# Two attentions under one gate: exps of the second by a polynomial of degree two, and V products that may begin with 128 columns

## The chip, the core and the metric

The kernel runs on one core of a Trainium2 chip. The metric is the device time of one execution in microseconds (us). A core has TensorE (PE in the profile; PEld is its weight load), VectorE (DVE), ScalarE (ACT), GpSimd (POOL) and SyncE (SP), which run their own instruction streams in order and wait for each other by semaphores. PE writes to PSUM alone, which the kernel divides into four slots of 128 x 1024 float32.

## The reference

```python
def _A_ref(x, wq, wk, wv, wo):            # 32 heads of q, one head of k and v, head size 16
    q = (x @ wq).reshape(B, S, H, Dh).transpose(0, 2, 1, 3)
    k = x @ wk
    v = x @ wv
    p = softmax(einsum("bhqd,bkd->bhqk", q, k) * Dh ** -0.5)
    return einsum("bhqk,bkd->bhqd", p, v).transpose(0, 2, 1, 3).reshape(B, S, H * Dh) @ wo

def _B_ref(x, wqkv, wo):                  # 32 heads of q, k and v
    q, k, v = (x @ wqkv).reshape(B, S, 3, H, Dh).transpose(2, 0, 3, 1, 4)
    p = softmax(einsum("bhqd,bhkd->bhqk", q, k) * Dh ** -0.5)
    return einsum("bhqk,bhkd->bhqd", p, v).transpose(0, 2, 1, 3).reshape(B, S, D) @ wo

g = sigmoid((x * gate_w).sum(-1, keepdims=True))
return g * _A_ref(x, ...) + (1 - g) * _B_ref(x, ...)
```

S = 2048 tokens, D = 512, 32 heads of 16, float32, one batch; both attentions read the same x. The weights are normal with deviation 0.05 (wq and wk of A times 8), so B's scaled scores are small numbers around zero.

## The kernel before

**The work.** Scores are made transposed, keys on partitions, queries on columns, so that exps can go straight into the product with V without a transpose. The work is cut into 8 groups (A and B in turn, eight heads each), and each group into four *phases* (half of the queries, half of the heads): 32 phases. A phase has 32 *quads* (`QUADS`), one for 128 keys and half of the placement in PE's rows; a quad has two *scores*, each 128 x 1024 in one PSUM slot (`products`, eight matmuls of 512 columns that run side by side in PE's sub-arrays). That gives 2048 scores. Each is turned into exps of 128 x 1024 by one instruction, and the quad's two tiles then go through the V product (`values`) into the phase's accumulator, `pair[0]`. The V product of a quad has 512 columns and may be issued in pieces of 128, 256, 384 or 512 (`value_job`). V has a column of ones beside it, so that the row sums of the softmax come out of the same product.

**Who makes exps.** ACT makes most of them (L793). For the others (`vector_job`, `chain`) DVE makes them by arithmetic. For A it goes through the bits of the float and a polynomial (`convert`, `mantissa`, `power`, four times `horner`: five full passes and two at half the time). For B, whose scores are small, it uses a polynomial of degree three in three full passes (`first`, `second`, `third`; L1049, L1052, L1056), with a second tile "w".

**The slots.** One slot is `pair[0]`. Other work that needs PSUM (projections of q, k and v, the output product, turning V, a score for DVE) takes the free slot that `hold()` puts into `pair[1]`; `release()` gives it back. `free["spare"]` is when that slot is free again, and `current` the unit of other work that is under way. Scores for ACT use what is left.

**What sets the order.** Nothing is scheduled at run time. While the program is built, a planner (`_Plan`, `pe_step`) keeps a clock for each engine with rough costs (`EXP`, `PRODUCT`, `SCORES`) and decides what PE issues next: a score, if a slot is free and ACT will want it; or a piece of a V product, or a job of a unit, if it fits in the time until the next score is wanted (`limit`). DVE's work goes into a list (`plan.vec`) with a rank and a due time and comes out by rank. The numbers `CHAIN`, `WORK`, `BEGIN` and the due times only change that order.

**After a phase** (`emptied`, `normalised`): DVE copies the accumulator out (L917), the row sums travel over DRAM into a compact tile (`held`, then `each`, on SP's queue), DVE inverts them and multiplies by the gate (`gated`, L674 and L675), they are spread back by DMA, and DVE multiplies, rounds and splits the result (`times`, `high`, `low`). The output product (`o_unit`) adds two phases of A and two of B; its sums go to DRAM and are added up there.

**The flag.** The fast path is only right for inputs in a range. `stats` gathers maxima; `flag_reduce` and `flag_check` make a flag from them near the end; if it is set, a slow general version runs after.

**The end.** After the last phase the sums are handled by `over`, `times`, `high`, `low` and `products_of` in four pieces of 128 queries, and `give` adds the product to the output row and stores it (L1545). Two of the eight rows go another way: ACT scales them (`added`, L1550) and GpSimd's queue adds them into DRAM.

```python
    def value_job(now, mine, room):
        ...
        m, n = going[mine] if mine in going else (min(can), 0)
        fit = int(min(room, 2 * HALF) // PRODUCT) * P
        wide = min(max(fit, BLK // 2), BLK - n)
```

## Time and profile before

| | |
|---|---|
| median of three runs | 1730.31 us (1729.32 to 1733.89) |
| the profiled execution | 1731.76 us, span 1729.9 us |
| busy | PE 1687.4, PEld 1008.2, DVE 1487.2, ACT 1665.2, POOL 195.5 us |
| first exp starts, last exp starts | 28.2 and 1702.7 us |
| mean granted clock of TensorE | 0.994 |

In rows of groups the figures after `|` are busy us and the mean ns of one instruction, then the engine's idle time before them and what ended it. In rows of the timeline the first number is the start from the span's beginning, the second the length, both us; several instructions that follow each other are one row with their count. A float32 matmul stands in the trace as two, so 16 matmuls of a V product are one piece.

### The profile page before, as it was taken

The numbers are of one execution on the slowest core, as the hardware profiler recorded it, in microseconds if no ns is written. First come the engines' busy times: TensorE is split into PE (matmuls) and PEld (weight loads), VectorE is DVE, ScalarE is ACT, GpSimd is POOL, SyncE is SP. The second block draws the span as 40 slices with busy tenths as digits, with TensorE's granted clock in tenths as the row PEclk, the third lists the DMA queues.
The fourth block names the chain that finished last, engine by engine and source line by source line (L and its number), as shares of the span: only waits on it lengthen the run. The fifth ranks groups of instructions, "written<-read, shape, count | busy, mean of one in ns | idle before, by whom it ended". The sixth has DMA issues, their size and how long they took to land.

```text
span 1729.9 us, 110256 instructions
## 1 busy us (share of the span) xinstructions
PE 1687.4 (98%) x51451; PEld 1008.2 (58%) x51451; DVE 1487.2 (86%) x1658; ACT 1665.2 (96%) x1813; POOL 195.5 (11%) x316
## 2 busy tenths in 40 slices
PE   8999999999999999999999999999999999999996
PEld 5556546456566656666566555665665655655553
DVE  5567699999998899988999888999899898988954
ACT  4999999999999999999999999999999999999994
POOL 1111101000101200011111010111102111111000
PEclk9999999999999999999999999999999999999998
DMA  5212201111212211231222122222213212222312
GB/s 148 74 43 57 56 9 48 41 41 48 54 35 59 68 40 42 53 77 42 41 54 54 48 59 41 47 59 61 60 28 61 59 48 60 36 40 66 121 54 77
DMA packets 71446, 95.72 MB, mean 55 GB/s; under 512 B 27612, under 2 KB 36092, under 8 KB 70980
## 3 DMA queue, kind: packets, MB, share of 16 engines
q1 hardware_dynamic: 53892, 58.61, 12.7%
q0 software_dynamic: 13856, 27.74, 8.0%
q8 instruction: 405, 6.64, 1.6%
q10 hardware_dynamic: 3232, 2.23, 0.4%
q14 instruction: 61, 0.50, 0.1%
HBM read 23.45 MB, written 18.33 MB: 24 GB/s over the span
## 4 chain that ended last, share of the span: by engine, by line
PE 61%; ACT 18%; issue 12%; DVE 7%; DMA 1%; POOL 0%; SPq 0%; ACTq 0%; DVEq 0%; POOLq 0%
PE slot L847 32%; PE slot L762 17%; ACT prob L793 11%; PE slot L215 11%; ACT vec L793 6%; DVE prob L1049 1%; DVE prob L1056 1%; DVE prob L1052 1%; DVE vec L1029 1%; DVE vec L1049 1%; DVE vec L1052 1%; DMA Qa<-hiqa 0%; PE slot L1407 0%; PE slot L309 0%; DVE vec L1016 0%
## 5 line engine op out<-in xcount | busy, mean ns | idle before, releaser
L793 ACT ACTIVATE prob<-slot 128x1024 f32<-128x1024 f32 x1129 | 1121.4, 1101 | 19.3 <-PE slot L762 14.7
L793 ACT ACTIVATE vec<-slot 128x1024 f32<-128x1024 f32 x657 | 685.6, 1099 | 7.6 <-PE slot L762 3.6
L847 PE MATMUL slot<-prob,vB 64*32 64x256 f32 (+3 forms) x8096 | 529.6, 439 | 0.1
L847 PE MATMUL slot<-prob,vA 64*32 64x512 f32 (+3 forms) x7536 | 499.1, 447 | 0.0
L762 PE MATMUL slot<-Qa,kA 64*32 64x512 f16 x8192 | 441.6, 378 | 8.4 <-DMA Qa<-hiqa 2.0
L762 PE MATMUL slot<-Qb,K 64*32 64x512 f16 x8192 | 421.2, 378 | 12.7 <-ACT prob L793 4.6
L847 PE MATMUL slot<-vec,vB 64*32 64x512 f32 (+3 forms) x4640 | 367.8, 434 | 0.8 <-issue 0.7
L847 PE MATMUL slot<-vec,vA 64*32 64x512 f32 (+3 forms) x4656 | 365.7, 446 | 0.0
L762 PEld LDWEIGHTS <-K 64*32 64x32 f16 x8192 | 192.4, 90 | 239.9 <-issue 191.3
L762 PEld LDWEIGHTS <-kA 64*32 64x32 f16 x8192 | 191.8, 90 | 235.4 <-issue 180.8
L847 PEld LDWEIGHTS slot<-prob,vB 64*32 64x32 f32 x8096 | 214.9, 106 | 38.8 <-issue 8.5
L847 PEld LDWEIGHTS slot<-prob,vA 64*32 64x32 f32 x7536 | 199.8, 106 | 43.4 <-issue 14.0
L847 PEld LDWEIGHTS slot<-vec,vB 64*32 64x32 f32 x4640 | 144.7, 106 | 26.6 <-issue 8.3
L847 PEld LDWEIGHTS slot<-vec,vA 64*32 64x32 f32 x4656 | 140.2, 106 | 26.4 <-issue 8.3
L1049 DVE TENSOR_SCALAR prob<-slot 128x1024 f32<-128x1024 f32 x109 | 133.0, 1220 | 17.9 <-PE slot L762 15.1
L1029 DVE SCALAR_TENSOR_TENSOR prob<-prob,prob 128x1024 f32<-128x1024 f32 x83 | 101.1, 1220 | 1.0
L1049 DVE TENSOR_SCALAR vec<-slot 128x1024 f32<-128x1024 f32 x71 | 86.6, 1220 | 12.4 <-PE slot L762 8.2
L215 PEld LDWEIGHTS <-o 64*32 64x32 f16 x3072 | 56.5, 93 | 32.8 <-ACT o L694 6.8
L1016 DVE TENSOR_SCALAR prob<-slot 128x1024 int32<-128x1024 f32 x46 | 56.2, 1221 | 19.4 <-PE slot L762 17.0
L1052 DVE SCALAR_TENSOR_TENSOR prob<-prob 128x1024 f32<-128x1024 f32 x59 | 71.5, 1219 | 0.5
L1056 DVE SCALAR_TENSOR_TENSOR prob<-prob,prob 128x1024 f32<-128x1024 f32 x59 | 71.5, 1218 | 0.2
L1029 DVE SCALAR_TENSOR_TENSOR prob<-prob,vec 128x1024 f32<-128x1024 f32 x55 | 67.0, 1220 | 0.7
(190 smaller groups left out, 1748.5 us busy)
## 6 DMA issues: line engine op xcount, KB each, us to landing
vB<-vB SPq DMA_DIRECT2D x32, 192.0 KB
prob<-back SPq DMA_DIRECT2D x184, 32.0 KB
out_dram<-vec POOLq DMA_DIRECT2D x36, 128.0 KB, 4.7
xT<-out_dram SPq DMA_DIRECT2D x16, 256.0 KB
out_dram<-prob POOLq DMA_DIRECT2D x28, 128.0 KB, 4.3
out_dram<-prob SPq DMA_DIRECT2D x24, 128.0 KB
out_dram<-xT SPq DMA_DIRECT2D x12, 256.0 KB
vec<-in_A_x_dram SPq DMA_DIRECT2D x10, 256.0 KB
```

The costliest lines, as they stand in the source:

```text
L215: nc.tensor.matmul(outs[n : n + COLS, i], lhs[i][rows(i), n : n + COLS], rhs[i][rows(i)], start=start, stop=stop)
L762: nc.tensor.matmul(bank[a : a + COLS, hh], k[rows(hh), key : key + COLS], Q[src, gi, half, p][rows(hh), j * BLK : (j + 1) * BLK], start=Tr ...
L793: nc.scalar.activation(probs[u], sc, AF.Exp, scale=SCALE / (UP * UP))
L847: nc.tensor.matmul(pair[0][32 * k : 32 * k + 32, i, cols], v[rows(i)], probs[2 * m + k // 2][rows(i), hh, cols], start=first, stop=last)
L1016: nc.vector.tensor_scalar(tile("p").bitcast(I32), pair[1], SCALE / (UP * UP) / math.log(2) * 2.0 ** 23, None, op0=ALU.mult)
L1029: nc.vector.scalar_tensor_tensor(p, m if i == 3 else p, VEC[i], m if i else w, op0=ALU.add, op1=ALU.mult)
L1049: nc.vector.tensor_scalar(tile("p"), pair[1], CUBE[0] * SCALE / (UP * UP), CUBE[1], op0=ALU.mult, op1=ALU.add)
L1052: nc.vector.scalar_tensor_tensor(tile("w"), tiles["p"], CUBE[2], tiles["p"], op0=ALU.add, op1=ALU.mult)
L1056: nc.vector.scalar_tensor_tensor(p, w, CUBE[3], p, op0=ALU.add, op1=ALU.mult)
```

## The change

Six things change.

1. **B's exps on DVE** become a polynomial of degree two in two passes: the score is scaled to p, and then (p + constant) x p is made. The polynomial's constant, about 1, is left out of the tile. The tile "w" is no longer needed. Only in the last phase is the constant added by a pass of its own (`third`).
2. **The constant comes back later.** For each half of a V projection, `sums_of` sums v over each 64 keys (a reduction from PSUM, a small multiplication, two transfers). When a B phase is normalised, `missing` adds up the sums of those quads that DVE made; `gated` adds the count to the row sums and `times` adds the sum to the result.
3. **The limit.** B's scores must stay under 0.044 instead of 0.16, so the bound is now by norms: `norms` squares q and k of B (before, `magnitudes` took magnitudes of q alone) and a small matmul adds them by head; `flag_pairs` multiplies the largest norms of q and k by head. This makes 16 such jobs instead of 8; B's k loses its plain maximum.
4. **V products** may begin with 128 columns, where before a first piece had at least 256, if the slot of other work is taken and no unit is under way (`least`).
5. **Numbers of the planner** change: `CHAIN` 28000 for A, `WORK` 500, `BEGIN` 4, tiles kept free, due times and earliest starts.
6. **The end**: all eight rows of the last part go through `give`; `added` is gone.

In the built order the counts are:

| | before | after |
|---|---|---|
| exps on ACT | 1796 | 1766 |
| exps on DVE: B, A | 180, 72 | 228, 54 |
| V products: pieces of 128, 256, 384, 512 columns | 330, 420, 330, 484 | 525, 475, 479, 296 |
| norm jobs on PE (L522, now L564) | 8 | 16 |

PE, in a phase of A near the beginning. `Qa00` are queries, `kA` keys, `slot` the PSUM slots, `vA` V, `prob` and `vec` the exps; one V piece is two rows. Before, a piece of 256 columns that begins a quad:

```order
L215 LDWEIGHTS w16vb01_780
L215 MATMUL slot3_82<-xT_83,w16vb01_780 32x512
L847 MATMUL slot2_81<-prob6_102,vA0_88 32x256 x4
L847 MATMUL slot2_81<-vec0_106,vA0_88 32x256 x4
L762 LDWEIGHTS kA_87
L762 MATMUL slot0_79<-Qa002_363,kA_87 32x512
```

and after, a place where a quad's last 256 columns are followed by the first 128 of the next, and then by a score:

```order
L816 LDWEIGHTS kA_87
L816 MATMUL slot1_80<-Qa002_366,kA_87 32x512
L901 MATMUL slot3_82<-vec4_110,vA1_89 32x256 x4
L901 MATMUL slot3_82<-vec3_109,vA1_89 32x256 x4
L901 MATMUL slot3_82<-vec2_108,vA0_88 32x128 x4
L901 MATMUL slot3_82<-prob0_96,vA0_88 32x128 x4
L816 LDWEIGHTS kA_87
L816 MATMUL slot2_81<-Qa003_367,kA_87 32x512
```

The interval between two scores there holds three units of 128 columns; before, a remainder of one unit could not be filled by a new quad.

DVE, from the copy that empties the accumulator of the 13th phase, the first of the second group of B. `slot` to `prob` or `vec` begins a chain. Before, the next 24 rows up to `gated` (L674) begin

```order
L917 COPY prob2_98<-slot1_80 128x1024
L1049 TENSOR_SCALAR vec2_108<-slot2_81 128x1024
L1052 SCALAR_TENSOR_TENSOR prob5_101<-vec2_108 128x1024
L1056 SCALAR_TENSOR_TENSOR vec2_108<-prob5_101,vec2_108 128x1024
L1049 TENSOR_SCALAR prob3_99<-slot3_82 128x1024
L247 TENSOR_SCALAR w16oa10_18034<-woa1_18032 128x512
L1052 SCALAR_TENSOR_TENSOR vec3_109<-prob3_99 128x1024
L250 SCALAR_TENSOR_TENSOR w16oa10_18034<-woa1_18032,w16oa10_18034 128x512
```

and after, all rows up to `gated` (L724 adds the count to `each`, L725 inverts it) are

```order
L972 COPY prob9_105<-slot1_80 128x1024
L1104 TENSOR_SCALAR prob7_103<-slot2_81 128x1024
L1107 SCALAR_TENSOR_TENSOR prob7_103<-prob7_103 128x1024
L1104 TENSOR_SCALAR prob2_98<-slot2_81 128x1024
L225 TENSOR_REDUCE stats_86<-w16kb20_18695 128x1
L1107 SCALAR_TENSOR_TENSOR prob2_98<-prob2_98 128x1024
L569 TENSOR_REDUCE stats_86<-slot2_81 64x1
L248 TENSOR_SCALAR w16ob10_18920<-wob1_18918 128x512
L545 TENSOR_REDUCE lost300_18975<-sums1_15233 64x1 x2
L724 TENSOR_SCALAR each300_18962<-each300_18962 128x32
L725 RECIPROCAL each300_18962<-each300_18962 128x32
```

Chains are two rows long instead of three, and `gated` has moved from the 24th row behind the copy to the ninth.

DVE at the very end, `give` in before (L1545) and after (L1620):

```order
L689 SCALAR_TENSOR_TENSOR vec1_107<-vec1_107 128x128
L1545 SCALAR_TENSOR_TENSOR xT_83<-slot1_80,gate_up_95,xT_83 128x512
L697 TENSOR_TENSOR o16712_43733<-vec1_107,o16712_43733 128x128
L689 SCALAR_TENSOR_TENSOR vec1_107<-vec1_107 128x128
L1545 SCALAR_TENSOR_TENSOR xT_83<-slot1_80,gate_up_95,xT_83 128x512
L697 TENSOR_TENSOR o16712_43733<-vec1_107,o16712_43733 128x128
L1545 SCALAR_TENSOR_TENSOR xT_83<-slot3_82,gate_up_95,xT_83 128x512 x2
L1545 SCALAR_TENSOR_TENSOR xT_83<-slot2_81,gate_up_95,xT_83 128x512 x2
```

```order
L1620 SCALAR_TENSOR_TENSOR xT_83<-slot3_82,gate_up_95,xT_83 128x512
L751 TENSOR_TENSOR o16712_45360<-vec2_108,o16712_45360 128x128
L740 SCALAR_TENSOR_TENSOR vec2_108<-vec2_108 128x128
L1620 SCALAR_TENSOR_TENSOR xT_83<-slot3_82,gate_up_95,xT_83 128x512
L751 TENSOR_TENSOR o16712_45360<-vec2_108,o16712_45360 128x128
L1620 SCALAR_TENSOR_TENSOR xT_83<-slot0_79,gate_up_95,xT_83 128x512 x2
L1620 SCALAR_TENSOR_TENSOR xT_83<-slot2_81,gate_up_95,xT_83 128x512 x2
L1620 SCALAR_TENSOR_TENSOR xT_83<-slot1_80,gate_up_95,xT_83 128x512 x2
```

The first two `give` now read the tile of the first 128 queries, which was ACT's; two more stand at the end.

The diff, cut to its core (line numbers of before are in the kernel above):

```diff
-B_MAX = 0.16
+B_MAX = 0.044
-CUBE = (0.5500864384102879, 0.8808852829622843, -0.986763876, 1.22848465)
+SQUARE = (1.0000001191795511, 1.0002430729569356, 0.4999387172344313)
...
             one = plan.vec(hi, 1130, 1, t + TO_VEC)
+            if part == "v":
+                one = plan.vec(blocks, 1250, 0, 0.0, (one,))
             plan.vec(lo, 1130, 0, 0.0, (one,), then)
...
+    def sums_of(gi, half):
+        if half == 0:
+            v_sums[gi] = ops.tile([P, 2, 2 * NT], F32, tag="sums", name=f"sums{gi}", bufs=2)
+        at = slice(NT * half, NT * (half + 1))
+        own, other = v_sums[gi][:, 0, at], v_sums[gi][:, 1, at]
+        nc.vector.tensor_reduce(own, pair[1].rearrange("p e (n k) -> p (e n) k", k=ROWS), axis=AX.X, op=ALU.add)
+        nc.vector.tensor_scalar(own, own, SQUARE[0] * UP ** -2, None, op0=ALU.mult)
+        swapped(other, own, nc.sync)
+        plan.sp += 2 * ISSUE_SP
...
+    def missing(ph, to):
+        n, half, q = phases[ph]
+        sums = v_sums[n // 2]
+        taken = [divmod(m - 32 * ph, 2) for m in range(32 * ph, 32 * ph + 32) if m in vector]
...
+                nc.vector.tensor_reduce(to[rows(i), r : r + 1], sums[rows(i), i ^ (q // 2), a:b], axis=AX.X, op=ALU.add)
...
-        nc.vector.tensor_scalar(mag.bitcast(I32), hi.rearrange("p e t -> p (e t)").bitcast(I32), 0x7FFF7FFF, None, op0=ALU.bitwise_and)
+        nc.vector.tensor_scalar(mag, hi, -HI_MAX, HI_MAX, op0=ALU.max, op1=ALU.min)
+        nc.vector.scalar_tensor_tensor(mag, mag, SQUARED / (UP * UP), mag, op0=ALU.mult, op1=ALU.mult)
...
         def gated():
+            if short:
+                count = missing(ph, lost)
+                nc.vector.tensor_scalar(each, each, SQUARE[0] * ROWS * count, None, op0=ALU.add)
             nc.vector.reciprocal(each, each)
...
-        plan.vec(gated, 430, 3.5, now + 7500, (), spreads, min(due, now + 25000),
+        plan.vec(gated, 900 if short else 430, 3.5, now + 7500, (), spreads, min(due, now + 35000),
...
-        wide = min(max(fit, BLK // 2), BLK - n)
+        least = P if n == 0 and free["spare"] > now and not current else BLK // 2
+        wide = min(max(fit, least), BLK - n)
...
             def first():
-                nc.vector.tensor_scalar(tile("p"), pair[1], CUBE[0] * SCALE / (UP * UP), CUBE[1], op0=ALU.mult, op1=ALU.add)
+                nc.vector.tensor_scalar(tile("p"), pair[1], math.sqrt(SQUARE[2]) * SCALE / (UP * UP), None, op0=ALU.mult)
             def second():
-                nc.vector.scalar_tensor_tensor(tile("w"), tiles["p"], CUBE[2], tiles["p"], op0=ALU.add, op1=ALU.mult)
+                nc.vector.scalar_tensor_tensor(tiles["p"], tiles["p"], SQUARE[1] / math.sqrt(SQUARE[2]), tiles["p"], op0=ALU.add, op1=ALU.mult)
             def third():
-                p, w = tiles["p"], tiles["w"]
-                nc.vector.scalar_tensor_tensor(p, w, CUBE[3], p, op0=ALU.add, op1=ALU.mult)
-                give("w")
+                nc.vector.tensor_scalar(tiles["p"], tiles["p"], SQUARE[0], None, op0=ALU.add)
...
-    CHAIN = 14000, 7000
-    JOB, AFTER, TURN, WORK = 500, 3000, 3000, 2500
+    CHAIN = 28000, 7000
+    JOB, AFTER, TURN, WORK = 500, 3000, 3000, 500
...
+    def flag_pairs():
...
-        elif t == 2:
-            give(1, 0)
         else:
-            give(1, 1)
+            give(0, t - 2)
         low[t]()
         products_of(t)
-        if t in (1, 2):
-            added(0, t - 1)
-    for t in (2, 3):
+    for t in range(1, 4):
         for e in range(2):
             give(t, e)
```

## The prediction

> **What bounds the kernel now.** I read the page first, then the busy times of the stretch in which exps run, then the timeline of single stretches, and last the groups by form. The page:

> ```profile
> span 1729.9 us, 110256 instructions
> ...
> PE 1687.4 (98%) x51451; PEld 1008.2 (58%) x51451; DVE 1487.2 (86%) x1658; ACT 1665.2 (96%) x1813; POOL 195.5 (11%) x316
> ...
> PEclk9999999999999999999999999999999999999998
> ```

> TensorE (PE) and ScalarE (ACT) both look full, VectorE (DVE) nearly so; a busy PE is not a PE at its peak, so the 98% decides nothing. The view of stretches and the source view of the exp line give the stage that matters, from the first exp to the end of the last; the columns of the stretch are span, then busy us and count of PE, PEld, DVE, ACT and POOL.

> ```profile
> 28.20:1703.80 1675.60, 1654.51 (x50809) 989.20 (x50817) 1462.39 (x1602) 1655.08 (x1797) 189.04 (x302) 1.00 0.22 52
> ```

> ```profile
> L793 ACT ACTIVATE prob<-slot x1129: 1016/1103/1257, 28.2 to 1702.7; 128x1024 f32<-128x1024 f32 x189
> L793 ACT ACTIVATE vec<-slot x657: 1014/1103/1223, 37.9 to 1700.8; 128x1024 f32<-128x1024 f32 x165
> ```

> ACT is busy for 1655.1 of 1675.6 us. With ten more into borrowed tiles (`early`, `vB`) its exps are 1796. What one costs, and what PE's work costs, is read from a piece of timeline near the end where both run without a gap:

> ```profile
> 1698.14 1.97 ACT L793 ACTIVATE prob<-slot 128x1024 f32<-128x1024 f32 x2
> 1699.94 2.00 ACT L793 ACTIVATE vec<-slot 128x1024 f32<-128x1024 f32 x2
> 1701.75 2.02 ACT L793 ACTIVATE prob<-slot 128x1024 f32<-128x1024 f32 x2
> ```

> ```profile
> 1700.31 0.41 PE L762 MATMUL slot<-Qb,K 64*32 64x512 f16 x8
> 1700.53 0.85 PE L847 MATMUL slot<-prob,vB 64*32 64x384 f32 x16
> 1701.17 0.42 PE L762 MATMUL slot<-Qb,K 64*32 64x512 f16 x8
> 1701.39 0.85 PE L215 MATMUL slot<-w16oa,o 64*32 64x512 f16 x24
> 1702.04 0.42 PE L762 MATMUL slot<-Qb,K 64*32 64x512 f16 x8
> 1702.25 0.42 PE L847 MATMUL slot<-prob,vB 64*32 64x128 f32 x16
> 1702.47 1.07 PE L847 MATMUL slot<-vec,vB 64*32 64x512 f32 x16
> 1703.33 1.07 PE L847 MATMUL slot<-prob,vB 64*32 64x512 f32 x16
> ```

> Two exps take 1.805 us from start to start (1698.14 to 1699.94 to 1701.75), so one costs 0.903; I use 0.905. PE works in units: a score is one (1700.31 to 1700.53, 0.22), a projection or output step one (24 matmuls in 0.65 are three), 128 columns of a V product one (1702.25 to 1702.47, 0.22; 384 columns 0.64; 512 columns 0.86). I use 0.2155 a unit. Counted in the built order, before has 2048 scores, 4096 units of V and 1158 jobs of other work (some 30 of them counted as two or three units by their matmuls): 7349 units, 1583 us. ACT's 1796 exps are 1625 us. In 1675.6 us ACT thus loses 50 us and PE 92. ACT is the bound; PE is 4.09 units an exp, 0.882 us against 0.905, close behind. Where ACT loses its 50 us the table of waits names PE:

> ```profile
> ACT prob L793 <- PE slot L762: 14.7, 19, 6.4
> ...
> ACT vec L793 <- PE slot L762: 3.6, 10, 0.8
> ```

> That is ACT waiting for a score that PE gave late; the rest are smaller delays.

> **The exps.** Of 2048 exps, DVE makes 252 before (180 of source B, 72 of A). In the built order after, it makes 228 of B and 54 of A, 282, and ACT 1766. ACT loses 30 exps: 30 x 0.905 = 27.2 us less. This lies on the path.

> **DVE.** What it pays, by the groups:

> ```profile
> L1049 DVE TENSOR_SCALAR prob<-slot 128x1024 f32<-128x1024 f32 x109 | 133.0, 1220 | 17.9 <-PE slot L762 15.1 <-ACT prob L793 1.8 <-ACT vec L793 0.7
> ...
> L1052 DVE SCALAR_TENSOR_TENSOR prob<-prob 128x1024 f32<-128x1024 f32 x59 | 71.5, 1219 | 0.5
> ...
> L1020 DVE TENSOR_SCALAR prob<-prob 128x1024 int32<-128x1024 int32 x29 | 20.1, 691 | 0.6
> ...
> L224 DVE TENSOR_REDUCE stats<-hikb 128x1 f32<-128x1024 f16 x8 | 9.7, 1208 | 0.0
> ```

> ```profile
> L516 DVE TENSOR_SCALAR vec<-hiqb x5: 417/418/421, 178.4 to 1576.2; 128x512 int32<-128x512 int32 x5
> ```

> A B chain falls from three passes of 1.22 to two; an A chain stays at five of 1.22 and two of 0.69. Full passes: 180 x 3 + 72 x 5 = 900 before, 228 x 2 + 54 x 5 = 726 after, -174 x 1.22 = -212 us; 36 fewer of 0.69, -25. Added: the constant's own pass for six exps of the last phase (L1110), 4 us at 0.69; eight reductions for the V sums, 10 us at 1.21; eight more norm reductions against eight fewer maxima of k, nothing. The two new passes over 16 norms against eight of 0.42 are not in the trace: between 0.42 + 1.22 (nearest row: the same bytes) and 2 x 1.22 each, 23 to 36 us; I take 23. The small sums of the missing constant: 15 times some four operations, each at most the 0.35 of L674's row below, so 0 to 21 us; I take 10. Together some -190, so DVE goes to about 1300 of 1487 us. None of that is a gain by itself: the cover is that a score whose exp DVE makes is asked for ahead of need. The eight more norm jobs each hold a PSUM bank for a unit and a reduction; the scores keep the two that they have in such a hold anyway, so I cost that at nothing beyond the units. If the cover goes, ACT waits (third rival).

> **PE gives some back.** Work stays (7357 units, with eight more norm jobs), so it is now 4.17 units an exp, 0.898 us against 0.905. To price it I split the built order at every eighth score that goes to ACT and took for each stretch the larger of 8 x 0.905 and its units x 0.2155. The sum is 1642.2 before and 1622.6 after, -19.6. Split at every third score, which leaves nearly no buffer, it is 1666.3 and 1654.1, -12.3; at every 64th, -23.5; ACT alone, -27.2. The measured 1675.6 lies above all of these, so what is between is lost in either kernel to waits that the count doesn't know. I take -19.6, since stretches of 8, 5 and 16 agree within 2 (-20.2 at 5, -21.2 at 16), and keep -12 and -27 as ends. The shorter first piece of V is in these counts: 525 pieces of 128 columns instead of 330, 1775 pieces instead of 1564. Intervals between two scores with exactly four units grow from 870 to 1083, those with five or more fall from 567 to 483.

> Does a piece cost more than its columns? The row at 1702.25 says not: 0.22 us for 128 columns, a quarter of 0.86. [...]

> **The late `gated`.** After each phase DVE copies the accumulator out, the row sums travel by DMA (`held`, then `each`), and DVE inverts them (L674). Before, in a B phase:

> ```profile
> 719.08 1.23 DVE L917 COPY prob<-slot 128x1024 f32<-128x1024 f32 x1 [0.38 <-PE slot L847]
> ...
> 745.37 0.35 DVE L674 RECIPROCAL each<-each 128x32 f32<-128x32 f32 x1
> ```

> Here 25 us of chain work stand between. In the order after, at the same phase, nine operations stand there, four full passes of 1.22, a reduction of 1.21 and small ones, some 7 us. The transfer has no other cover, and DVE runs in order, so it may stand idle. One event of before shows the price:

> ```profile
> 1558.92 0.35 DVE L674 RECIPROCAL each<-each 128x32 f32<-128x32 f32 x1 [2.86 <-DMA each<-held]
> ```

> ```profile
> 1557.74 1.03 ACT L793 ACTIVATE prob<-slot 128x1024 f32<-128x1024 f32 x1
> 1560.73 1.02 ACT L793 ACTIVATE vec<-slot 128x1024 f32<-128x1024 f32 x1 [1.96 <-DVE prob L1056]
> 1562.45 1.03 ACT L793 ACTIVATE prob<-slot 128x1024 f32<-128x1024 f32 x1 [0.69 <-PE slot L762]
> 1564.15 1.02 ACT L793 ACTIVATE prob<-slot 128x1024 f32<-128x1024 f32 x1 [0.68 <-PE slot L762]
> 1565.71 1.02 ACT L793 ACTIVATE prob<-slot 128x1024 f32<-128x1024 f32 x1 [0.53 <-PE slot L762]
> ```

> Four exps took 7.97 us (1557.74 to 1565.71) instead of 3.62, 4.35 lost. In all of before DVE waited for this transfer twice among 31 inversions, 3.2 us together (a row of the view of tile `each`):

> ```profile
>   DMA each<-held: 3.2, 2
> ```

> So most waits should be short and hidden by the score that lies ready; I take +1 in all, between 0 and 4.35 for each of 15 phases. The 16 new transfers of V sums on SP, 0.58 of issue each by the row of that queue below, are used a phase or more later: nothing, unless they push `each` back, which is the same rival. The two transfers for the flag (about 10 of its small operations on DVE) have 40 us of distance planned: nothing.

> **The tail.** Two output rows that ACT and GpSimd made are made by DVE now.

> ```profile
> 1715.67 0.69 ACT L1550 ACTIVATE prob<-slot,gate_up 128x512 f32<-128x512 f32 x1 [0.40 <-PE slot L215]
> ...
> 1716.95 0.75 DVE L1545 SCALAR_TENSOR_TENSOR xT<-slot,gate_up,xT 128x512 f32<-128x512 f32 x1 [0.81 <-PE slot L215]
> ...
> 1718.88 2.72 DVE L1545 SCALAR_TENSOR_TENSOR xT<-slot,gate_up,xT 128x512 f32<-128x512 f32 x4
> ```

> ```profile
> 1710.50 0.58 SPq L659 DMA_DIRECT2D vec<-prob  x1
> ```

> Two more of 2.72 / 4 = 0.68 are +1.36; the wait of 0.81 goes, since the tile that DVE now takes first was ready for ACT at 1715.67. Net +0.5. Two more issues on SP (0.58) run beside them. The wider bound is -0.8 to +1.4.

> **The sum.** -19.6 + 1.0 + 0.5 = -18.1. The profiled execution took 1731.8 us, 1.9 of them around its span; less 18.1 it is 1713.7. It lies 1.5 above the median of the three runs (1730.3), so a median near 1712. A change under 0.3% (5.2 us) can't be told from none.

> **Rivals.**
> First, PE becomes the bound outright: it keeps the 92 us that it loses now and gets 8 more units (+1.7), with the tail +0.5: 1730.3 + 2.2 = 1732.5, the same. For it speaks that 0.898 is within 1% of 0.905; against it that much of those 92 us is the remainder of 0.905 after four units (0.043 each), and that fewer intervals are now uneven.
> Second, weight loads no longer hide behind short pieces. The weight load's mean is 106 ns in

> ```profile
> L847 PEld LDWEIGHTS slot<-prob,vB 64*32 64x32 f32 x8096 | 214.9, 106 | 38.8 <-issue 8.5 <-ACT prob L793 0.4 <-DVE prob L917 0.4
> ```

> and one bare load for each of 211 more pieces is 22 us: 1712 + 22 = 1734, the same. The row at 1702.25 speaks against it.
> Third, slower: DVE waits for `each` in the B phases. Its place is the new `gated` ahead of which 7 us of work stand, its price 4.35 an event; from 1712 it needs six events of the 15 to pass 1735.5, and seven give 1742. For it speaks the lost 25 us of cover; against it that two waits in 31 inversions is all that before shows, and that DVE has spare time to catch up.
> Fourth, better: the event at 1558 does not come back (-4.35) and the 128 columns fill what PE lost, so the full -27.2 stands: 1699.
> That the fast path is left for the general one can be excluded: with these inputs the largest scaled product of a head's norms is 0.039, under the new limit of 0.044.

> **Chances.** Forecast (1703 to 1722) 0.70, PE bound 0.08, weight loads 0.04, DVE waits 0.08, better 0.10. Faster 0.80, same 0.12, slower 0.08. The range leaves out the slower rival and the two at 1732 to 1734: 1699 to 1723.

> **What the profile after would show.** ACT with 1766 exps at 0.905 and a stretch from first to last exp near 1657 us; DVE near 1300 us busy; V pieces of 128 columns still at 0.22 from start to start; DVE's waits for `each` under 1 us apiece; last exp to end 26.5 us instead of 26.1. I am wrong if ACT's waits for PE's scores grow by more than 10 us, if pieces of 128 columns are spaced wider, or if the waits for `each` reach ACT.

## The result and the profile after

The changed kernel is slower: 1742.93 us (median of 8 runs, 1738.28 to 1749.26) against 1730.64 (8 runs on the same chip), a ratio of 1.0065 with a 95% interval of 1.004 to 1.0089. Forecast were 1712 us and a range of 1699 to 1723. The profiled execution took 1745.55 us. Runs in which TensorE was granted a lower mean clock than the usual 0.992 to 0.997 took longer (of e10 below, one at 0.986 took 1710 us and the others 1692 to 1697), and e11 can't be understood without that.

The page of the changed kernel, the parts on busy time, on DMA queues and on the chain that ended last:

```profile
span 1743.7 us, 116765 instructions
...
PE 1694.9 (97%) x54859; PEld 1109.9 (64%) x54859; DVE 1336.7 (77%) x1568; ACT 1654.0 (95%) x1781; POOL 194.1 (11%) x314
...
PEclk9999999999999999999999999999999999999998
...
q8 instruction: 431, 7.06, 1.7%
...
PE 83%; ACT 7%; DVE 5%; issue 2%; DMA 1%; SPq 0%; ACTq 0%; DVEq 0%
```

The same two parts of the page of before, which the prediction did not look at:

```profile
q8 instruction: 405, 6.64, 1.6%
...
PE 61%; ACT 18%; issue 12%; DVE 7%; DMA 1%; POOL 0%; SPq 0%; ACTq 0%; DVEq 0%; POOLq 0%
```

ACT and DVE did what was forecast: 1766 exps on ACT instead of 1796, and the durations of all DVE instructions add up to 1402 us instead of 1584 (busy time counts overlapping ones once, so it fell by 150 only). But TensorE has 3408 matmuls and as many weight loads more, and the chain that ended last now runs over PE for 83% of the span instead of 61%. ACT's waits, of the table of waits (total, times, longest):

```profile
ACT prob L847 <- PE slot L816: 24.5, 46, 5.2
ACT vec L847 <- PE slot L816: 13.5, 28, 1.5
```

These are 38.0 us in 74 waits for scores, where before had 18.3 in 29. From the starts of the exps: beyond 0.904 an exp ACT lost 51.7 us between its first and last exp before, and 94.2 after. That is 42.5 more: it eats up the 27.2 us of the 30 exps and 15 us besides. No single event stands out. By size, the delays of 0.1 to 0.3 us add 18 us (156 instead of 44), those of 0.3 to 1 us 21 (75 instead of 35) and longer ones 5.

How PE came to be late stands in a piece of the timeline, in source A:

```profile
1307.23 1.23 PE L901 MATMUL slot<-prob,vA 64*32 64x512 f32 x16
...
1308.09 0.59 PE L816 MATMUL slot<-Qa,kA 64*32 64x512 f16 x8
1308.30 0.83 PE L901 MATMUL slot<-prob,vA 64*32 64x384 f32 x11
1308.84 1.03 ACT L847 ACTIVATE prob<-slot 128x1024 f32<-128x1024 f32 x1
1310.20 0.52 PE L901 MATMUL slot<-prob,vA 64*32 64x384 f32 x3 [1.06 <-issue]
...
1311.32 1.02 ACT L847 ACTIVATE vec<-slot 128x1024 f32<-128x1024 f32 x1 [1.45 <-PE slot L816]
```

A V product of 384 columns stops in its middle, after 11 of its 16 matmuls, and goes on at 1310.20 with no releaser named but "issue". One such place proves little, since the program has a few waits inside pieces too. The records of queue q8 show what else happens there: a packet of 16 KB starts at 1306.94 and lands at 1308.90, 1.30 us before PE goes on. All packets of q8 are 16384 bytes: 7.06 MB in 431. For 2 x 54859 weight loads and matmuls that is 64.4 bytes each, and before it was 64.5 (405 packets for 2 x 51451). So a packet would hold some 254 instructions of TensorE; I take blocks of 256, which e4 below shows by its stops. That makes 26 blocks more after. Between 100 and 1700 us there are 72 places where over 0.5 us lie from one matmul's start to the next; 42 of them end 1.25 to 1.75 us after such a block landed; before it was 12 of 52. By chance it would be about one in eight, for blocks come 4.0 us apart on average after and 4.25 before.

That gives the theory: **TensorE can be short of instructions.** Blocks seldom come closer than some 3.4 us (1% of the distances are under 3.33 us and 5% under 3.44 after, 3.38 and 3.50 before), so there are seldom more than about 75 instructions a us. A score or a step of other work has 16 instructions in 0.2155 us, 74 a us; a V piece has 32 whatever its width, so 512 columns are 37 a us, 256 are 74, and 128 are 149. A score and 384 columns fill 0.862 us with 48 instructions; a score, 128 and 256 columns fill the same time with 80, which is 93 a us. The rivals: the new order is worse for another reason (norm jobs, limits of the planner, bank holds), and the blocks only stand by; a piece has a fixed price, such as a weight load that is not hidden; DVE's waits for the row sums.

### The profile page after: what moved, and what is told of

Read it like the earlier page. It is cut to its first block, busy times and chain, and to the rows that moved or that the text cites. A ratio compares the mean times of both kernels' runs of the same rounds, so it can differ in the third digit from the quotient of the medians.

```text
span 1743.7 us, 116765 instructions
## 1 busy us (share of the span) xinstructions
PE 1694.9 (97%) x54859; PEld 1109.9 (64%) x54859; DVE 1336.7 (77%) x1568; ACT 1654.0 (95%) x1781; POOL 194.1 (11%) x314
## 3 DMA queue, kind: packets, MB, share of 16 engines
q8 instruction: 431, 7.06, 1.7%
## 4 chain that ended last, share of the span: by engine, by line
PE 83%; ACT 7%; DVE 5%; issue 2%; DMA 1%; SPq 0%; ACTq 0%; DVEq 0%
PE slot L901 45%; PE slot L816 23%; PE slot L216 14%; ACT prob L847 4%; ACT vec L847 3%; DVE prob L1104 1%; DVE vec L1104 1%; DVE prob L1107 1%; SPq L702 0%; DVE vec L1107 0%; PE slot L1482 0%; DMA each<-held 0%; PE slot L587 0%; DVE xT L1620 0%; DMA vec<-in_A_x_dram 0%
## 5 line engine op out<-in xcount | busy, mean ns | idle before, releaser
L847 ACT ACTIVATE prob<-slot 128x1024 f32<-128x1024 f32 x1091 | 1072.6, 1064 | 30.7 <-PE slot L816 24.5
L847 ACT ACTIVATE vec<-slot 128x1024 f32<-128x1024 f32 x665 | 676.7, 1061 | 20.3 <-PE slot L816 13.5
L901 PE MATMUL slot<-prob,vB 64*32 64x128 f32 (+3 forms) x8960 | 540.7, 402 | 4.2 <-issue 3.6
L901 PE MATMUL slot<-prob,vA 64*32 64x128 f32 (+3 forms) x8544 | 518.9, 419 | 1.8 <-issue 1.8
L816 PE MATMUL slot<-Qa,kA 64*32 64x512 f16 x8192 | 494.8, 378 | 6.4 <-issue 1.9
L901 PE MATMUL slot<-vec,vB 64*32 64x384 f32 (+3 forms) x5696 | 400.2, 401 | 1.3 <-issue 1.0
L901 PE MATMUL slot<-vec,vA 64*32 64x128 f32 (+3 forms) x5080 | 360.6, 414 | 1.6 <-issue 1.1
L901 PEld LDWEIGHTS slot<-prob,vB 64*32 64x32 f32 x8960 | 255.1, 106 | 53.2 <-issue 15.3
L901 PEld LDWEIGHTS slot<-prob,vA 64*32 64x32 f32 x8544 | 235.8, 106 | 45.9 <-issue 17.3
L901 PEld LDWEIGHTS slot<-vec,vB 64*32 64x32 f32 x5696 | 179.0, 106 | 30.5 <-issue 10.0
L1107 DVE SCALAR_TENSOR_TENSOR prob<-prob 128x1024 f32<-128x1024 f32 x146 | 178.5, 1223 | 3.2
L901 PEld LDWEIGHTS slot<-vec,vA 64*32 64x32 f32 x5080 | 160.7, 106 | 27.3 <-issue 8.7
L1104 DVE TENSOR_SCALAR vec<-slot 128x1024 f32<-128x1024 f32 x82 | 100.0, 1220 | 13.6 <-PE slot L816 10.8
L1107 DVE SCALAR_TENSOR_TENSOR vec<-vec 128x1024 f32<-128x1024 f32 x82 | 100.3, 1223 | 1.7
L1084 DVE SCALAR_TENSOR_TENSOR prob<-prob,prob 128x1024 f32<-128x1024 f32 x71 | 86.8, 1222 | 1.6
L216 PE MATMUL slot<-w16ob,o 64*32 64x512 f16 x1536 | 65.3, 391 | 5.6 <-ACT o L748 5.1
```

The source lines that it names most:

```text
L216: nc.tensor.matmul(outs[n : n + COLS, i], lhs[i][rows(i), n : n + COLS], rhs[i][rows(i)], start=start, stop=stop)
L816: nc.tensor.matmul(bank[a : a + COLS, hh], k[rows(hh), key : key + COLS], Q[src, gi, half, p][rows(hh), j * BLK : (j + 1) * BLK], start=Tr ...
L847: nc.scalar.activation(probs[u], sc, AF.Exp, scale=SCALE / (UP * UP))
L901: nc.tensor.matmul(pair[0][32 * k : 32 * k + 32, i, cols], v[rows(i)], probs[2 * m + k // 2][rows(i), hh, cols], start=first, stop=last)
L1084: nc.vector.scalar_tensor_tensor(p, m if i == 3 else p, VEC[i], m if i else w, op0=ALU.add, op1=ALU.mult)
L1104: nc.vector.tensor_scalar(tile("p"), pair[1], math.sqrt(SQUARE[2]) * SCALE / (UP * UP), None, op0=ALU.mult)
```

## Experiments

### The rule alone, undone and done

e1 is the changed kernel without the short beginning; e2 is the kernel before with it and nothing else.

```diff
 e1 (from the changed kernel)
-        least = P if n == 0 and free["spare"] > now and not current else BLK // 2
+        least = BLK // 2
 e2 (from the kernel before)
+        least = P if n == 0 and free["spare"] > now and not current else BLK // 2
-        wide = min(max(fit, BLK // 2), BLK - n)
+        wide = min(max(fit, least), BLK - n)
```

> The changed kernel with the one rule undone that lets a V product begin with 128 columns: it begins with 256 again. In the built order 1620 pieces of V instead of 1775 (1564 before), ACT with 1772 exps instead of 1766. Instruction theory: the extra pieces cost TensorE instructions, not columns; with them gone some 412 instruction blocks of 16 KB instead of 431, ACT's waits for PE's scores back near 20 us, and the sum of the prediction holds: 1710 to 1722 us. Rival, the new order as a whole (norm jobs, shorter chains, limits of the planner) is worse and the blocks only stand by: 1738 to 1748, as with the rule. Rival, waits of DVE for the row sums: also 1738 to 1748.

> The kernel before with that one rule added and nothing else: 1735 pieces of V instead of 1564, ACT's 1796 exps as before. Instruction theory: slower than before by 5 to 25 us, some 426 blocks instead of 405, and ACT's waits for PE's scores at 30 us or more instead of 18. Rival, the new order as a whole: 1726 to 1734, no change. By columns alone (the prediction's step): no change or a little faster, since TensorE fills time that it lost.

Measured: e1 1733.26 us, ratio to before 1.0002 (0.9988 to 1.0016); e2 1784.75 us, 1.0295 (1.0264 to 1.0325). The short beginning by itself costs 50 us in the old order and some 10 in the new one. The direction is the instruction theory's: e2 fetched 426 blocks, and ACT's waits for scores went from 18.3 to 44.5 us. The 50 us are twice the most that was expected, so a count of blocks alone doesn't give the price. e1 does not fit: it should have gained 10 to 20 us, and gained nothing. ACT has 24 exps fewer there and loses 73.5 us beyond 0.904 an exp instead of 51.7. The page and the waits of e1:

```profile
PE 1690.3 (98%) x52379; PEld 1019.9 (59%) x52379; DVE 1332.8 (77%) x1574; ACT 1646.5 (95%) x1787; POOL 190.9 (11%) x314
...
q8 instruction: 412, 6.75, 1.7%
```

```profile
ACT prob L847 <- PE slot L816: 22.1, 30, 5.3
...
ACT vec L847 <- PE slot L816: 6.1, 15, 0.9
ACT prob L847 <- PE slot L901: 5.0, 4, 1.7
...
ACT vec L847 <- PE slot L901: 3.0, 2, 1.5
```

The waits for scores are 28.2 us, ten more than before, with 7 blocks more. The last two rows have grown: ACT waits for V products (L901) to empty its tiles, 8.0 us in 6 waits against 2.5 in 2 before and 3.7 in 6 after. Three of them, of 1.5 us, come in source-A phases some 417 us apart (at 617, 1034 and 1451 us), where a phase ends just as a q projection has filled the other bank: V stands until DVE has copied the accumulator. A second loss follows each some 10 us later, and the six together cost ACT 11 us. That comes of the order, and it takes a part of the gain that e1 should have had. The third rival of the prediction shows up here once as well: before the last inversion, at 1662.6 us, DVE waits 7.5 us for `each`, and 5 us later ACT waits 3.0 us for `back`, the transfer that follows.

### More instructions, nothing else

e3 and e4 keep the order of before and every column where it was; V pieces are only issued in shorter calls.

```diff
-            values(m, slice(n, n + wide))
 e3: 384 columns as 128 and 256
+            cuts = [n, n + P, n + wide] if wide == 3 * P else [n, n + wide]
+            for x, y in zip(cuts, cuts[1:]):
+                values(m, slice(x, y))
 e4: all pieces as 128
+            for x in range(n, n + wide, P):
+                values(m, slice(x, x + P))
```

> The kernel before in its own order, each V piece of 384 columns issued as 128 and 256 back to back: same columns, same places, 330 more pieces, some 10600 more TensorE instructions, some 41 more blocks. Instruction theory: at least 12 us slower, ACT's waits for PE's scores doubled. Columns alone: 1728 to 1733, no change. A bare weight load a piece: 330 x 0.106, 35 us slower.

> The kernel before in its own order, every V piece issued as pieces of 128 columns: 4096 pieces instead of 1564, some 184000 TensorE instructions instead of 103000, about 719 blocks. Instruction theory: blocks come no faster than one in about 3.4 us (the shortest distances in the traces of before and after), so 719 x 3.4 = 2440 us. Columns alone: 1731 us. A bare weight load a piece: 2532 x 0.106 = 268, about 2000 us.

Measured: e3 1802.42 us (1.0412, 1.0384 to 1.0441), e4 2778.53. "Columns alone" is dead: the same columns in the same places cost 1044 us more in e4 (one run, at a clock of 0.986, against 1734.08 of before on the same chip). In e3 ACT's waits for scores went from 18.3 us in 29 to 61.1 in 106. The instruction theory had the direction; for e4 it said 2440 us, for it reckoned 3.4 us a block, and the 721 blocks came 3.84 us apart on average. The timeline of PE in e4 shows the mechanism by itself:

```profile
1504.89 0.27 PE L847 MATMUL slot<-vec,vA 64*32 64x128 f32 x1 [1.58 <-issue]
1504.90 0.31 PE L847 MATMUL slot<-prob,vA 64*32 64x128 f32 x4
1504.93 0.45 PE L762 MATMUL slot<-Qa,kA 64*32 64x512 f16 x4
1505.03 0.29 PE L847 MATMUL slot<-prob,vA 64*32 64x128 f32 x4
1505.14 0.60 PE L762 MATMUL slot<-Qa,kA 64*32 64x512 f16 x11
1505.37 0.27 PE L847 MATMUL slot<-prob,vA 64*32 64x128 f32 x2
1505.38 0.38 PE L762 MATMUL slot<-Qa,kA 64*32 64x512 f16 x1
1505.38 0.70 PE L847 MATMUL slot<-prob,vA 64*32 64x128 f32 x26
1505.84 0.42 PE L762 MATMUL slot<-Qa,kA 64*32 64x512 f16 x4
1505.90 0.30 PE L847 MATMUL slot<-prob,vA 64*32 64x128 f32 x4
1506.01 0.40 PE L762 MATMUL slot<-Qa,kA 64*32 64x512 f16 x4
1506.06 0.79 PE L847 MATMUL slot<-prob,vA 64*32 64x128 f32 x32
1506.73 0.41 PE L762 MATMUL slot<-Qa,kA 64*32 64x512 f16 x8
1506.95 0.62 PE L847 MATMUL slot<-vec,vA 64*32 64x128 f32 x23
1508.64 0.62 PE L847 MATMUL slot<-vec,vA 64*32 64x128 f32 x26 [1.07 <-issue]
```

Add the counts from one "issue" row to the row ahead of the next: 128 matmuls, so with their weight loads 256 instructions, one block. PE runs them in 2.7 us and stands until the next is there, 3.75 us after the last; both stops cut a piece in two. Of the 682 gaps over 0.5 us in e4, 509 end 1.25 to 1.5 us after a block landed, and 542 of the 681 stretches between them have exactly 128 matmuls. The gaps add up to 1064 us, about what e4 lost. Of the two queues of kind "instruction" only q8 grew in e4, from 405 to 721 packets (q14 has 61 in both); for the 2532 x 32 instructions that the edit gave TensorE that is 63.9 bytes each.

**A sum with instructions.** The prediction's count can now be mended. Over stretches of four ACT scores take the largest of 4 x 0.905, units x 0.2155 and instructions x 3.8 / 256 us, and add up. The 3.8 is e4's; the four was chosen because it fits the six stretches of exps known by then (unlike the prediction's count it leaves out the work behind the last full stretch, so its level is some 7 to 10 us lower):

| | before | after | e1 | e2 | e3 | e4 |
|---|---|---|---|---|---|---|
| blocks counted | 398 | 425 | 406 | 420 | 440 | 715 |
| without instructions, us | 1644 | 1625 | 1633 | 1647 | 1644 | 1644 |
| with them, us | 1668 | 1695 | 1667 | 1717 | 1746 | 2708 |
| measured, first to last exp's start, us | 1674 | 1690 | 1675 | 1727 | 1742 | 2715 |

Without the third term it gives the prediction's gain, 19 us; with it, a loss of 27, where 15 were measured. The sign does not hang on the four: counted again in the built order at stretches of 3, 5, 8 and 16, the loss is 27, 29, 22 and 25. It has e1 level with before, as was measured. The next runs tested it on kernels that it had not seen.

### Where instructions are added

All three keep the order of before.

```diff
 e5: scores of source A in two halves of 256 columns, 16 matmuls instead of 8
+                step = BLK // 2 if src == "a" else BLK
+                for x in range(0, BLK, step):
+                    nc.tensor.matmul(bank[a : a + COLS, hh, x : x + step], ...
 e6 (w = 4) and e7 (w = 2): pieces of 512 or of 256 columns in two halves
+            step = wide // 2 if wide == w * P else wide
+            for x in range(n, n + wide, step):
+                values(m, slice(x, x + step))
```

> The kernel before in its own order; each score of source A is issued as 8 matmuls of 256 columns and 8 more of the other 256, so 16 weight loads and 16 matmuls instead of 8 and 8. V pieces are untouched; 16400 more TensorE instructions, 64 more blocks. Instruction theory, by a sum over stretches of four ACT scores, each the largest of 4 x 0.905, units x 0.2155 and instructions x 3.8 / 256 us (it gives 1668, 1695, 1667, 1717, 1746, 2708 for the stretch of exps of before, after, e1, e2, e3 and e4, where 1674, 1690, 1675, 1727, 1742, 2715 were measured): +160, about 1890 us. Theory that a V piece has a fixed price of about 0.2 us, whatever its neighbours: no change, 1731. Columns alone: 1731.

> The kernel before in its own order; each V piece of 512 columns is issued as 256 and 256: 484 more pieces, 61 more blocks, and in the place where they lie TensorE has at most 74 instructions a us. Instruction theory by the sum: +91, about 1822 us. Fixed price of a piece (70 us for 330 pieces in e3, 0.21 each): +103, 1833; this run alone tells little between the two, the pair with the next one does. Columns alone: 1731.

> The kernel before in its own order; each V piece of 256 columns is issued as 128 and 128: 420 more pieces, 53 more blocks, fewer than in the run before. Instruction theory by the sum: +146, about 1877 us, dearer than the run before though fewer pieces are added, because these double the instructions where TensorE has 149 a us. Fixed price of a piece: 420 x 0.21 = +88, 1819, cheaper than the run before. Columns alone: 1731.

Measured: e5 1901.24 us, e6 1825.20, e7 1848.01, against 1731.96 before: +169, +93 and +116 where the sum said +160, +91 and +146. e5 touches no V piece and costs the most, so it is no price of V pieces. e7 adds fewer pieces than e6 and costs more, so a piece had no fixed price: it cost 0.19 us in e6, whose halves have 74 instructions a us by the count above, and 0.28 in e7, whose halves have 149. The waits of e7:

```profile
ACT prob L793 <- PE slot L762: 69.1, 102, 6.2
...
ACT vec L793 <- PE slot L762: 29.7, 53, 1.3
```

### A cheaper order that was not

```diff
 e8 (from the changed kernel)
-LEFT, LEFT_END, BEGIN = 1, 1, 4
+LEFT, LEFT_END, BEGIN = 2, 1, 4
...
-        least = P if n == 0 and free["spare"] > now and not current else BLK // 2
+        least = BLK // 2
```

> The changed kernel with V beginning with 256 columns, and two spare tiles instead of one kept back before a burst of other work: 1577 pieces, 401 blocks, ACT with 1786 exps. Instruction theory by the sum: 1664 for the stretch of exps against 1668 of before, so 1724 to 1731 us. By the prediction's count without instructions: 1637 against 1644, about the same gain, so this run only asks whether a cheaper order beats both kernels.

Measured: 1739.80 us, ratio 1.0045 (1.0029 to 1.006): a miss by 9 to 16 us. The sum knows no banks and no full tiles; in e8 ACT waits for V products again, 5.3 us in 6 waits, and for scores 28.2. Differences under some 12 us are beyond it. Of the runs with all products, none beats the kernel before.

### Fewer instructions

If instructions are the limit, the change should pay once they are not. In these kernels the V products of the second 64 rows are left out, except in the first and last quad of a phase. The two row halves run side by side: in before, the 512 columns at 1702.47 are eight matmuls and, 0.43 us later, eight more; in e9 the 512 columns at 1670.88 are four and, also 0.43 us later, four more. So the columns of the first 64 rows and their places stay, and a V piece has 16 instructions instead of 32. e9 is before, e10 after, e11 is e1 and e12 is e2, all with this edit.

```diff
-            for i in range(2):
+            for i in range(2 if put_in[0] in (0, QUADS - 1) else 1):
```

> The kernel before in its own order, but in all V quads of a phase except the first and the last, the products of the second 64 rows are left out. The two row halves run beside each other on TensorE, so a piece should still take 0.2155 us per 128 columns with half the instructions: some 307 blocks instead of 398. Instruction theory by the sum: 1655 instead of 1668 for the stretch of exps, about 1718 us. Columns alone: 1731. It is the base for the next two.

> The changed kernel with the same products left out: some 321 blocks instead of 425. Instruction theory by the sum: 1634 for the stretch, 21 below the run before, so about 1697 us: the gain that was predicted comes out once instructions don't limit. Rival, the new order itself is worse: 10 to 15 us above the run before, as it is with all products.

> The changed kernel with V beginning with 256 columns and the same products left out: 311 blocks. Instruction theory by the sum: 1643, 12 below e9 and 9 above e10, so about 1706 us: the short beginning, which costs 10 with all products, gains here. Rival, the order: level with e9, as it is with all products.

> The kernel before with the short beginning alone (as in e2) and with the V products of the second 64 rows left out as in e9. With all products the short beginning cost 2.95%. Instruction theory by the sum: 1659 for the stretch of exps against 1655 in e9, so about 1722 us, a ratio of 0.993 to the kernel before where e9 had 0.9905. Rival, the order that the short beginning makes is bad in itself: some 50 us above e9, a ratio near 1.02.

| | median us | ratio to before | interval | with all products |
|---|---|---|---|---|
| e9 (before) | 1718.83 | 0.9905 | 0.9890 to 0.9921 | 1 |
| e10 (after) | 1694.61 | 0.9781 | 0.9751 to 0.9810 | 1.0065 |
| e11 (e1) | 1724.48 | 0.9905 | 0.9872 to 0.9938 | 1.0002 |
| e12 (e2) | 1726.57 | 0.9955 | 0.9939 to 0.9972 | 1.0295 |

e9 and e10 came within 3 us of what was expected, and e10 is 24.2 us faster than e9; expected were 21. The same change in the same order costs 12 us with 425 blocks and gains 24 with 321. So the order is not bad in itself, and the price of the short beginning in the old order falls from 50 us to 8 (e12 over e9, where the sum said 4 and the rival some 50). A rival would be that these kernels also relieve PE of columns, since the other 64 rows stand free. A score's matmuls do start earlier beside a V piece (after a piece of 512 columns the next operation starts at 0.72 us in e9 instead of 0.86), but PE goes through the columns of the first 64 rows no faster: over stretches of 100 units the quickest 1% take 0.215 us a unit in e9 and 0.214 in e10, against 0.217 before and 0.216 after. The page and the waits of e10:

```profile
PE 1655.3 (98%) x41539; PEld 991.6 (59%) x41539; DVE 1332.7 (79%) x1568; ACT 1634.7 (97%) x1781; POOL 194.0 (11%) x314
...
q8 instruction: 327, 5.36, 1.4%
```

```profile
ACT prob L847 <- PE slot L816: 8.3, 5, 6.0
ACT vec L847 <- PE slot L816: 2.5, 4, 1.0
```

74 waits for scores have become 9. e11 missed its 1706 us. By its median it is level with e9, as the rival had it. Four of its six runs had a granted clock of 0.986 or 0.987 and took 1724 to 1726 us; the two at 0.994 and 0.995, the clock of e9's runs, took 1712 and 1710, 7 to 9 below e9 and 15 to 17 above e10. The profiled one is of the four: its clock was down near the end (0.58 on average from 1645 to 1676 us). By the two runs alone the short beginning gains in the new order once instructions don't limit, but 11 of the 15 to 17 us are the losses around ends of phases that e1 has: they are still there in e11 (three of 1.74 us and three of 1.96), so they come of the order and not of instructions. In the old order the short beginning still costs 8 us. What it is worth by itself is thus not settled.

## Why the prediction was wrong

- **The exps and DVE: right.** 1766 ACT exps, 927 of them still 0.90 to 0.91 us behind the one ahead; DVE's durations fell by 182 us (forecast 190; its busy time is 1336.7 us, forecast near 1300), and none of it was a gain by itself.
- **"Does a piece cost more than its columns?": this step failed.** The prediction answered from the row at 1702.25, 0.22 us for 128 columns, that the 211 extra pieces were free. The row is right, and half of the 128-column pieces that run whole in the changed kernel still take 0.218 us or less, but it stands beside 512-column pieces, which need 37 instructions a us. What the pieces brought was 211 x 32 = 6752 instructions, 26 blocks of q8. The page of before had q8 with 405 packets, and the planner's `takes` counts 32 a piece and 16 a step against `BLOCK` and `READ` (256 and 3400 ns); either was a reason to count instructions as well as columns. (The planner's 3.4 us a block is itself too short: in e4 it was 3.84.)
- **"PE gives some back", -19.6: mis-sized for the same cause.** It took the larger of two terms where there are three. With the third it is +27 by the sum, +15 measured in the stretch, and +12.3 in the medians where the whole sum said -18.1. The gain that it named exists: 24 us between e9 and e10.
- **First rival, PE bound at 1732.5:** the engine was right (83% of the chain), the size not. It kept PE's loss of 92 us; PE's loss grew to 105 (1690.8 less 7357 units of 0.2155).
- **Second rival, weight loads no longer hidden, 1734:** its total was nearer than the forecast, its mechanism not. A bare load for each piece gives about 2000 us in e4 (2778 measured) and a price by the piece, which e6 against e7 excludes. Nor would e4's PE, at a price by the piece, run 128 matmuls in 2.7 us and then stand.
- **Third rival, waits for `each`:** they grew from 3.2 us in 2 to 9.4 in 8 on DVE and none was longer than 2.3, where seven events of 4.35 on ACT were needed. The rows of the changed kernel:

```profile
DVE each L724 <- DMA each<-held: 5.0, 5, 2.3
DVE each L725 <- DMA each<-held: 4.4, 3, 2.0
```

- **The signs named beforehand** did their work: "wrong if ACT's waits for PE's scores grow by more than 10 us" came true with 19.7. "If pieces of 128 columns are spaced wider" did not: they are not wider, they are cut.
- From the first exp's start to the last one's end it took 1690.8 us (forecast 1657), from there to the end 26.0 (forecast 26.5).

Not settled: how the misfit between sum and time in single kernels (12 to 15 us in the changed kernel, 30 in e7, 9 to 16 in e8) divides among banks, full tiles and the spread of block distances.

## What to carry to other kernels

Count an engine's instructions as well as its columns. Shorter pieces left the columns alone and added instructions, and here the rate of instructions was a bound of its own (e4: 2778 us instead of 1734 with the same columns), local to the places that were dense. In e4's trace its signs were a piece cut in its middle with "issue" as the only releaser, the same count of instructions between such stops (128 matmuls in 542 of 681 stretches), and a DMA queue of kind "instruction" whose packets landed 1.2 to 1.55 us ahead of most restarts. A price read in a sparse place did not hold in a dense one: 128 columns took 0.22 us beside a piece of 512, and issuing 420 pieces of 256 columns as two of 128 cost 116 us in e7.
